# Inner rows of a gated layer transposed by VectorE and placed by transfers, with one buffer for split queries and keys

## The chip, the core and the metric

The kernel runs on one core of a Trainium2 chip. The metric is the device time of one execution in microseconds. The engines are TensorE (PE; its weight loads are listed apart as PEld), VectorE (DVE), ScalarE (ACT), GpSimd (POOL) and SyncE (SP), which here only issues transfers.

## What is computed

Block-causal attention over 8 batches, 8 heads, 576 positions and 64 dimensions a head (blocks of 64), whose result, 4608 rows of 512, goes through a gated layer with 1024 inner columns:

```python
scores = scale * np.matmul(q, k.transpose(0, 1, 3, 2))
mask = block_i >= block_j
scores = np.where(mask, scores, -1000000000.0)
scores = scores - np.max(scores, axis=-1, keepdims=True)
attn = np.exp(scores)
attn = attn / (np.sum(attn, axis=-1, keepdims=True) + 1e-09)
out = np.matmul(attn, v)                      # then rows of all heads side by side: x
h = x @ w_in
e = np.exp(h - np.max(h, axis=-1, keepdims=True))
sm = e / (np.sum(e, axis=-1, keepdims=True) + 1e-09)
solu = h * sm
mu = np.mean(solu, axis=-1, keepdims=True)
var = np.mean((solu - mu) ** 2, axis=-1, keepdims=True)
ln = (solu - mu) / np.sqrt(var + 1e-06) * g_ln
return ln @ w_out
```

q, k and v are float32; w_in and w_out come as 64-bit floats, whose words the kernel turns into float32 itself.

## The kernel before, in words

Matmul operands are split into a high part (a copy rounded to the matmul's type) and a low part (the difference), and three products of parts are summed, so each product below is three matmuls. The work has two streams.

*Attention*, `attention(p)`, for 32 pairs of heads (4 pairs a batch). Keys and queries of a pair are loaded by four transfers each, in pieces of 32 floats, so that DVE's transpose of 32x32 blocks (L428) gives them with the head dimension on the partitions (`kt`, `qt`). ACT (or POOL) makes the high parts `kh`, `qh` (L429, L430), DVE the low parts `ql`, `kl` (L432, L434); these four exist twice, for even and odd pairs. POOL copies the last query block of both heads into a block-diagonal pair `qdh`, `qdl` (L439). Then come the scores on PE (64-row matmuls L458 for query blocks of 128, and L452 for the last blocks of both heads), DVE's row maxima (L481), ACT's exponentials with row sums (L485), the scaling by the reciprocal sums (L501 on POOL), 25 PE transposes of the probabilities (L512) with copies out of PSUM by ACT (L389), the product with the values (AV, L545) and its copies into `xt` (also L389), which holds three batches.

*The layer*, `moe(t, key)`, for 36 tiles of 128 rows. `xh`, `xl` are split from `xt` (L577, L581). H, the product with w_in, is two halves of 12 matmuls (L602) into one 1024-wide PSUM tile. DVE takes the maximum (L608), ACT the exponential into `u` (L609), DVE three small steps (L617 to L619) and the product with h into `u` (L610). `u` is centred (L612 on POOL or L613 on DVE), ACT squares it for the variance (L614, output into `junk`), and POOL makes the row factor (L625, L626). `u`, the inner rows, is transposed by PE, four 128x128 transposes a half (L637); ACT copies the high part `ch` out of PSUM (L641) and DVE subtracts the low part `cl` (L642). O, the product with w_out, is two halves of 12 matmuls (L650), ACT scales it into `ob` (L654), SP stores it (L656). `ub`, `ob` exist twice, `ch`, `cl` once.

The weights are made from their words in 16 pieces (`prep`), with temporaries in the third buffer of `xt`.

The order of each engine's instructions is written out by a planner, `Schedule.run`: a list scheduler over operations with assumed durations, latencies and priorities (`PARAMS`, one number for each kind of operation, added to the number of the pair or tile). It runs at build time; on the chip each engine works through its own list and waits on semaphores. `K["np"]` is the number of pairs, `e0`, `a_...` are penalties for letting another engine do an operation. PSUM is given out as two tiles of 1024 (kind D) and four of 512 (kind S).

Of the kernel before, what the change touches and what calls it, by code (L numbers as in the profile page):

```python
# [31 lines left out]
NPT = 2  # L32
SWITCH = 165.0
# [164 lines left out]
def kernel(  # L198
# [11 lines left out]
    K = PARAMS  # L210
# [16 lines left out]
    def sb(name, shape, dt=F32):  # L227
        return cp.tile([P] + shape, dt, name=name)
# [18 lines left out]
    qdh, qdl = ([sb(f"{x}{i}", [P], F32R) for i in range(2)] for x in ("qdh", "qdl"))  # L247
# [20 lines left out]
    xt = [sb(f"xt{i}", [NP, S]) for i in range(3)]  # L268
# [62 lines left out]
    xtf = xt[2].rearrange("p a b -> p (a b)")  # L331
    wtmp = [(xtf[:, 0:512], xtf[:, 512:1024], ob[0]), (xtf[:, 1024:1536], xtf[:, 1536:2048], ob[1])]
# [59 lines left out]
    def attention(p):  # L392
# [5 lines left out]
        half = [slice(0, 64), slice(64, 128)]  # L398
        for nm, src, dst in (("kz", k, kz), ("qz", q, qz)):

            def load(nm=nm, src=src, dst=dst):
                for g in range(4):
                    dma = ACT if p == 0 and nm == "kz" else SP
# [5 lines left out]
            op("SP", 1600, load, w=[nm], key=(K["l0"] if p == 0 else p) + K["ld" + sfx], tail=2400)  # L409
# [122 lines left out]
        x2 = wkeys if b0 == 2 else []  # L532
# [22 lines left out]
        for ph in range(2):  # L555
            av = avs[ph]
            for rows, parts in xparts[ph]:
                for c_, q_, l_ in parts:
                    copy(2, l_, lambda rows=rows, av=av, c_=c_, q_=q_, l_=l_: (xt[b0 % 3][rows, hp, q_ : q_ + l_], PS(av)[rows, c_ : c_ + l_]), 1.0, [("xt", b0 % 3, hp, rows.start, q_)], ke, av, x2)


    def moe(t, key):
# [51 lines left out]
        op("ACT", t_act(1024, 135), lambda: ACT.activation(junk, u, AF.Square, accum_out=m[:, 4:5]), r=[uk], w=[("m4", i)], key=key + K["sq"])  # L614
# [86 lines left out]
```

## Time and profile before

| what | value |
|---|---|
| median of 3 runs | 790.3 us (789.97 to 790.9) |
| the profiled execution | 790.35 us, its span (first to last instruction) 788.6 us |
| PE, PEld busy | 760.3 us, 595.4 us |
| DVE, ACT, POOL busy | 471.7, 521.6, 341.7 us |
| mean granted TensorE clock | 0.975 |
| transfers | 47.05 MB in 198,551 packets |

The busy time of PE is the union of records that overlap; what an instruction adds to the run is read from the chain of work that ended last, whose pieces follow each other without overlap. A group's mean duration is that of one record. Idle time of an engine counts only where that engine is what the others wait for. "Granted clock" is the share of full TensorE speed that the chip allowed in a stretch.

### The profile page before, as it was taken

The page shows a single profiled execution, that of the slowest core. Times are in us where ns is not written, and L with a number is a line of the kernel's source. Part 1 is how long each engine was busy: PE and PEld are TensorE (multiplying, and loading weights), DVE is VectorE, ACT ScalarE, POOL GpSimd, SP SyncE. Part 2 cuts the span into 40 slices and gives each one's busy share as a digit, 9 for nine tenths or more (in the row PEclk, how much of TensorE's full clock was granted, in tenths as well). Part 3 has the DMA queues.
Part 4 walks back from the last instruction along what each step waited for, and adds up shares of the span by engine and source line. Part 5 has one row for each costly group of instructions (what it writes and reads, how often), then busy time and mean ns, then how long its engine had stood idle before and what let it go on. Part 6 is the DMA issues. An engine that isn't in the chain of part 4 may idle for free.

```text
span 788.6 us, 13834 instructions
## 1 busy us (share of the span) xinstructions
PE 760.3 (96%) x4687; PEld 595.4 (76%) x4687; DVE 471.7 (60%) x1191; ACT 521.6 (66%) x1349; POOL 341.7 (43%) x593
## 2 busy tenths in 40 slices
PE   4878999999999999999999999999999999999998
PEld 3656776887777777777777777787777878888886
DVE  5889998955666555555555666655554534444442
ACT  5788989876677676666777667677666654443332
POOL 4766857645444444444444444444445131121100
PEclk8787999999999999999999999999999999999999
DMA  9764653322222222222222222222200100000001
GB/s 185 144 137 118 120 120 88 61 59 59 58 43 48 59 49 55 59 46 59 59 59 59 59 46 48 55 51 54 59 23 22 30 14 27 26 16 28 14 27 41
DMA packets 198551, 47.05 MB, mean 60 GB/s; under 512 B 191824, under 2 KB 191824, under 8 KB 198480
## 3 DMA queue, kind: packets, MB, share of 16 engines
q1 hardware_dynamic: 196112, 45.87, 26.9%
q8 instruction: 37, 0.61, 0.3%
q10 hardware_dynamic: 2368, 0.30, 0.3%
q14 instruction: 34, 0.28, 0.1%
HBM read 36.70 MB, written 9.44 MB: 59 GB/s over the span
## 4 chain that ended last, share of the span: by engine, by line
PE 86%; ACT 5%; DVE 4%; DMA 2%; issue 1%; POOL 1%; SPq 0%; DVEq 0%; ACTq 0%; POOLq 0%
PE ps L650 25%; PE ps L602 25%; PE ps L512 10%; PE ps L545 9%; PE ps L458 8%; PE ps L637 4%; PE ps L452 3%; ACT pb L485 2%; DVE nm L481 1%; DMA ub<-in_moe_w_out_dram 1%; DMA kz<-in_k_dram 1%; DMA ub<-in_moe_w_in_dram 1%; POOL pb L501 0%; ACT xt L389 0%; DVE ql L432 0%
## 5 line engine op out<-in xcount | busy, mean ns | idle before, releaser
L501 POOL TENSOR_SCALAR pb<-pb,rz 128x384 f32<-128x384 f32 (+4 forms) x288 | 176.6, 629 | 241.4 <-DVE rz L494 227.2
L485 ACT ACTIVATE pb<-ps,nm 128x256 f32<-128x256 f32 (+4 forms) x288 | 155.1, 548 | 47.3 <-DVE nm L481 46.6
L389 ACT ACTIVATE pt<-ps 128x512 f32<-128x512 f32 (+1 forms) x224 | 108.5, 562 | 42.0 <-PE ps L512 41.6
L642 DVE TENSOR_TENSOR cl<-ps,ch 128x512 fp32r<-128x512 f32 x72 | 49.4, 686 | 142.7 <-ACT ch L641 142.7
L481 DVE TENSOR_REDUCE nm<-ps 128x1 f32<-128x256 f32 (+4 forms) x288 | 131.4, 509 | 2.1 <-PE ps L452 2.1
L512 PE MATMUL ps<-ident,pb 128*128 128x128 f32 x800 | 111.2, 287 | 11.2 <-POOL pb L501 6.3
L512 PEld LDWEIGHTS ps<-ident,pb 128*128 128x128 f32 x800 | 93.9, 146 | 24.6 <-POOL pb L501 9.7
L545 PE MATMUL ps<-pt,vr 128*64 128x320 f32 (+4 forms) x896 | 93.8, 360 | 0.3 <-ACT pt L389 0.3
L545 PEld LDWEIGHTS ps<-pt,vr 128*64 128x64 f32 x896 | 59.3, 137 | 34.4 <-issue 1.3
L602 PE MATMUL ps<-wih,xh 128*128 128x512 f32 x288 | 84.7, 416 | 0.2 <-ACT pb L485 0.2
L650 PE MATMUL ps<-woh,ch 128*128 128x512 f32 x288 | 83.4, 411 | 0.0
L602 PE MATMUL ps<-wil,xh 128*128 128x512 f32 x288 | 79.8, 399 | 0.0
L650 PE MATMUL ps<-wol,ch 128*128 128x512 f32 x288 | 79.0, 396 | 0.0
L602 PE MATMUL ps<-wih,xl 128*128 128x512 f32 x288 | 78.8, 395 | 0.0
L650 PE MATMUL ps<-woh,cl 128*128 128x512 f32 x288 | 78.6, 394 | 0.0
L625 POOL TENSOR_TENSOR ms<-ms,mhalf 128x1 f32<-128x1 f32 x36 | 19.8, 549 | 131.8 <-DVE ms L622 131.7
L641 ACT ACTIVATE ch<-ps 128x512 fp32r<-128x512 f32 x72 | 44.0, 611 | 49.5 <-PE ps L637 49.5
L458 PE MATMUL ps<-kh,qh 64*128 64x256 f32 (+3 forms) x256 | 57.4, 395 | 10.5 <-POOL qh L430 5.4
L602 PEld LDWEIGHTS ps<-wil,xh 128*128 128x128 f32 x288 | 54.9, 190 | 13.0
L654 ACT ACTIVATE ob<-ps,ms 128x512 f32<-128x512 f32 x36 | 24.8, 688 | 60.0 <-PE ps L650 54.3
L602 PEld LDWEIGHTS ps<-wih,xl 128*128 128x128 f32 x288 | 54.4, 189 | 12.9
L650 PEld LDWEIGHTS ps<-wol,ch 128*128 128x128 f32 x288 | 54.3, 188 | 12.8
(83 smaller groups left out, 1275.5 us busy)
## 6 DMA issues: line engine op xcount, KB each, us to landing
qz<-in_q_dram SPq DMA_DIRECT2D x128, 72.0 KB, 2.5
out_dram<-ob SPq DMA_DIRECT2D x36, 256.0 KB, 2.0
kz<-in_k_dram SPq DMA_DIRECT2D x124, 72.0 KB, 2.5
vr<-in_v_dram SPq DMA_DIRECT2D x64, 128.0 KB, 2.6
ub<-in_moe_w_in_dram SPq DMA_DIRECT2D x8, 512.0 KB, 4.2
ub<-in_moe_w_out_dram SPq DMA_DIRECT2D x8, 512.0 KB, 3.7
vr<-in_v_dram SPq DMA_DIRECT2D x32, 32.0 KB, 2.4
kz<-in_k_dram ACTq DMA_DIRECT2D x4, 72.0 KB, 3.8
```

The source lines that it names most:

```text
L389: op("ACT", t_act(n_), lambda: ACT.activation(aps()[0], aps()[1], AF.Copy, scale=scale), r=r, w=w, key=key, ps=ps, alts=[("DVE", t_dve(n_) ...
L458: PE.matmul(PS(sps[h])[:, off : off + 128 * (i_ + 1)], w_[half[h], 128 * i_ : 128 * i_ + 128], x_[half[h], 0 : 128 * (i_ + 1)], start=n_ = ...
L481: op("DVE", t_dve(wid[u]), lambda sp=sp, off=off, u=u: DVE.tensor_reduce(out=nm_[u], in_=PS(sp)[:, off : off + wid[u]], axis=AX.X, op=ALU. ...
L485: op("ACT", t_act(wid[u], 186), lambda sp=sp, off=off, u=u, zg=zg, zc=zc: ACT.activation(pb[:, poff[u] : poff[u] + wid[u]], PS(sp)[:, off ...
L501: op("POOL", 0.836 * nn + 243, lambda b=b, nn=nn, zg=zg, zc=zc: POOL.tensor_scalar(out=pb[:, poff[b] : poff[b] + nn], in0=pb[:, poff[b] : ...
L512: PE.transpose(t[:, (s_ - c0) * P : (s_ - c0 + 1) * P], pb[:, poff[b] + j * P : poff[b] + (j + 1) * P], ident)
L545: PE.matmul(PS(avs[ph])[half[h], 64 * o_ : 64 * (o_ + n_)], vt[:, j, 64 * h : 64 * h + 64], pt_.rearrange("p s q -> p (s q)")[:, 128 * s_ ...
L602: PE.matmul(o_, a_[:, c, :], w_[:, c, s_], start=(si == 0 and c == 0), stop=(si == 2 and c == NKI - 1))
L637: PE.transpose(t_[:, c * P : (c + 1) * P], u[:, (4 * hf + c) * P : (4 * hf + c + 1) * P], ident)
L641: op("ACT", t_act(512), lambda cs=cs, cps=cps: ACT.activation(ch[:, cs, :].rearrange("p c q -> p (c q)"), PS(cps), AF.Copy), w=[("ch", hf) ...
L642: op("DVE", t_dve(512), lambda cs=cs, cps=cps: DVE.tensor_tensor(out=cl[:, cs, :].rearrange("p c q -> p (c q)"), in0=PS(cps), in1=ch[:, cs ...
L650: PE.matmul(o_, a_[:, c, :], w_[:, c, :], start=(hf == 0 and si == 0 and c == 0), stop=(hf == 1 and si == 2 and c == 7))
```

## The change

The lines of the changed kernel are numbered anew: L602 and L650 (H and O) become L640 and L705, L637 becomes L693, L458, L452, L512, L545 become L497, L491, L551, L583, the loads L404 become L425 (L414 and L419 for the first four pairs).

For tiles 6 to 33 (`PET`, `PEL`) PE no longer transposes the inner rows. DVE transposes `u` in 32x32 blocks into `zb` (L670), SP moves the 16 groups of blocks to their places in `ct` by transfers of 32 partitions x 1 KB (L675), ACT copies the high part from `ct` (L683, other engines are allowed) and DVE subtracts (L686). `zb` and `ct` exist once. For the first four pairs (`PEQ`) queries and keys are loaded as they lie, in pieces of 64 floats, their last 64 positions together in `kq`, and transposed by PE (L454, L456); ACT and DVE split them from PSUM. The split queries and keys exist once (`NQK`). Square's output goes into `ob` instead of a buffer of its own, and the temporaries of `prep` lie in `zb` and `ct`. The priorities are new.

```diff
+NQK = 1
+XB = 3
+PEQ = 4
+PET, PEL = 6, 34
...
-    "nd": 2, "ld": -112.86, "lv": 9.571, "q": 88.586, "qe": 132.144, "s": 58.329, "se": -84.684,
+    "nd": 2, "ld": -183.871, "lv": -100.446, "q": -108.839, "qe": 198.742, "s": 92.976, "se": 35.817,
...
+    kq = sb("kq", [P])
-    qh, ql, kh, kl = ([sb(f"{x}{i}", [S], F32R) for i in range(2)] for x in ("qh", "ql", "kh", "kl"))
+    qh, ql, kh, kl = ([sb(f"{x}{i}", [S], F32R) for i in range(NQK)] for x in ("qh", "ql", "kh", "kl"))
...
+    zb = sb("zb", [DFF])
+    ct = sb("ct", [4, NKO, 32])
-    junk = sb("junk", [DFF], mybir.dt.bfloat16)
...
-    wtmp = [(xtf[:, 0:512], xtf[:, 512:1024], ob[0]), (xtf[:, 1024:1536], xtf[:, 1536:2048], ob[1])]
+    wtmp = [(zb[:, 0:512], zb[:, 512:1024], ob[0]), (ctf[:, 0:512], ctf[:, 512:1024], ob[1])]
...
+                if peq:
+                    for h in range(2):
+                        dma.dma_start(
+                            dst[:, 0:512].rearrange("p (c d) -> p c d", c=4)[:, :, 64 * h : 64 * h + 64],
+                            src[b0, 2 * hp + h, 0:512, :].rearrange("(c p) d -> p c d", p=P),
+                        )
...
+        if peq:
+            pq, pk = newps("S"), newps("D")
+
+            def trans(src, ps, tail):
+                for c in range(4):
+                    PE.transpose(PS(ps)[:, c * P : (c + 1) * P], src[:, c * P : (c + 1) * P], ident)
+                if tail:
+                    PE.transpose(PS(ps)[:, 4 * P : 5 * P], kq, ident)
...
+            copy(0, S, lambda: (kh_, PS(pk)[:, 0:S]), 1.0, [("kh", iq)], ke, pk)
+            copy(0, 512, lambda: (qh_[:, 0:512], PS(pq)[:, 0:512]), 0.125, [("qh", iq, 0)], ke, pq)
...
-        op("ACT", t_act(1024, 135), lambda: ACT.activation(junk, u, AF.Square, accum_out=m[:, 4:5]), r=[uk], w=[("m4", i)], key=key + K["sq"])
+        op("ACT", t_act(1024, 135), lambda: ACT.activation(ob[i].bitcast(mybir.dt.bfloat16), u, AF.Square, accum_out=m[:, 4:5]), r=[uk], w=[("m4", i), ("ob", i)], key=key + K["sq"])
...
+        if PET <= t < PEL:
+            op("DVE", t_dve(DFF), lambda: DVE.transpose(zb.rearrange("p (r c i) -> p r c i", r=4, i=32), u.rearrange("p (c r i) -> p r c i", r=4, i=32)), r=[uk] + (wkeys if t == PET else []), w=["zb"], key=key + K["ct"])
+
+            def place():
+                for r_ in range(4):
+                    for a_ in range(4):
+                        SP.dma_start(ct[32 * r_ : 32 * r_ + 32, a_, :, :], zb[32 * a_ : 32 * a_ + 32, 256 * r_ : 256 * r_ + 256])
+
+            op("SP", 2800, place, r=["zb"], w=["ct"], key=key + K["ct"], tail=2400)
...
+            if PET <= t < PEL:
+                c_ = ct[:, :, cs, :]
+                op("ACT", t_act(512), lambda c_=c_, h_=h_: ACT.activation(h_, c_, AF.Copy), r=["ct"], w=[("ch", hf)], key=key + K["ce"],
...
+                op("DVE", t_dve(512), lambda c_=c_, h_=h_, l_=l_: DVE.tensor_tensor(out=l_, in0=c_, in1=h_.bitcast(F32), op=ALU.subtract), r=["ct", ("ch", hf)], w=[("cl", hf)], key=key + K["ce"], port=True,
...
+                continue
```

How this moves instructions is seen at three places. First PE late in the program, where only tiles are left. Before, the second half of one tile's O, the next tile's first transposes, and so on (`ps` are PSUM tiles, `ub` the inner rows, `woh`, `wol` the parts of w_out, `x4` four instructions in a row):

```order
L650 MATMUL ps_65<-woh,ch 128x512 x4
L650 MATMUL ps_65<-wol,ch 128x512 x4
L650 MATMUL ps_65<-woh,cl 128x512 x4
L637 MATMUL ps_64<-ident,ub_133 128x128 x4
L650 MATMUL ps_65<-woh,ch 128x512 x4
L650 MATMUL ps_65<-wol,ch 128x512 x4
L650 MATMUL ps_65<-woh,cl 128x512 x4
L637 MATMUL ps_66<-ident,ub_133 128x128 x4
L602 MATMUL ps_62<-wih,xh_129 128x512 x4
```

And now, at the same stage:

```order
L705 MATMUL ps_63<-woh,ch 128x512 x4
L705 MATMUL ps_63<-wol,ch 128x512 x4
L705 MATMUL ps_63<-woh,cl 128x512 x4
L705 MATMUL ps_63<-woh,ch 128x512 x4
L705 MATMUL ps_63<-wol,ch 128x512 x4
L705 MATMUL ps_63<-woh,cl 128x512 x4
L640 MATMUL ps_61<-wih,xh_124 128x512 x4
```

The transposes are gone and both halves of O follow each other. Second, SP in the middle of the program, one round before (values, a result, keys, queries, values of the next pair):

```order
L413 DMA vr_82<-in_v_dram 128x4x64 x2
L417 DMA vr_82<-in_v_dram 64x2x64
L656 DMA out_dram<-ob_138 128x512
L404 DMA kz<-in_k_dram 32x18x32 x4
L404 DMA qz<-in_q_dram 32x18x32 x4
```

and now:

```order
L675 DMA ct<-zb 32x256 x16
L434 DMA vr_84<-in_v_dram 128x4x64 x2
L438 DMA vr_84<-in_v_dram 64x2x64
L425 DMA kz<-in_k_dram 32x18x32 x4
L425 DMA qz<-in_q_dram 32x18x32 x4
L711 DMA out_dram<-ob_134 128x512
```

Sixteen transfers stand in each round between a store and the loads of values. Third, DVE in the stage of tiles alone, from one tile's block transpose to the next one's (`ms` are row values, L646 and L648 the maximum and the product of the next tile, L651 its centring, L686 the subtractions for the tile before):

```order
L670 STREAM_TRANSPOSE zb<-ub_129 128x1024
L660 TENSOR_SCALAR ms_137<-ms_137 128x1
L646 TENSOR_REDUCE ms_136<-ps_61 128x1
L655 TENSOR_SCALAR ms_136<-ms_136 128x1
L656 RECIPROCAL ms_136<-ms_136 128x1
L657 TENSOR_SCALAR ms_136<-ms_136 128x1
L648 SCALAR_TENSOR_TENSOR ub_128,ms_136<-ps_61,ub_128 128x1024
L686 TENSOR_TENSOR cl<-ct,ch 128x4x4x32
L649 TENSOR_SCALAR ms_136<-ms_136 128x1
L651 TENSOR_SCALAR ub_128<-ub_128,ms_136 128x1024
L686 TENSOR_TENSOR cl<-ct,ch 128x4x4x32
L670 STREAM_TRANSPOSE zb<-ub_128 128x1024
```

The subtractions from `ct` now stand between the product and the block transpose of the next tile.

## Rows read from the trace of the kernel before

**Rows 1.** The page's part 1: busy time, share of the span, instructions.

```profile
PE 760.3 (96%) x4687; PEld 595.4 (76%) x4687; DVE 471.7 (60%) x1191; ACT 521.6 (66%) x1349; POOL 341.7 (43%) x593
```

**Rows 2.** Stretches: start:end length, busy PE, PEld, DVE, ACT, POOL, clock, DMA share, GB/s.

```profile
0.00:40.00 40.00, 27.06 (x156) 20.61 (x156) 28.73 (x68) 25.18 (x67) 23.88 (x56) 0.79 0.85 166
40.00:136.00 96.00, 84.49 (x556) 62.94 (x554) 87.33 (x216) 85.55 (x237) 65.68 (x99) 0.89 0.53 118
136.00:590.00 454.00, 454.00 (x2955) 356.23 (x2954) 272.17 (x715) 319.21 (x855) 210.46 (x369) 1.00 0.26 53
590.00:770.00 180.00, 180.00 (x959) 143.95 (x956) 79.17 (x185) 86.73 (x186) 40.94 (x69) 1.00 0.07 23
```

**Rows 3.** Groups: the inner transposes; x count | busy us, mean ns | idle before.

```profile
L637 PE MATMUL ps<-ident,ub 128*128 128x128 f32 x288 | 44.5, 277 | 0.0
```

**Rows 4.** Chain in order of time, one round: start us, us, what.

```profile
341.14 2.98 PE ps L602 x12
...
346.19 0.44 PE ps L637 x4
...
349.96 0.59 PE ps L637 x4
...
355.93 2.78 PE ps L602 x12
...
362.58 2.99 PE ps L602 x12
```

**Rows 5.** The same view, two tiles of the last stretch.

```profile
700.29 5.59 PE ps L602 x24
...
712.36 2.79 PE ps L602 x12
```

**Rows 6.** Waits: who waited for whom, us in total, times, longest.

```profile
PEld ps L458 <- issue: 24.0, 69, 0.4
```

**Rows 7.** Groups of ACT: exponentials, their accumulator reads, copies of transposed probabilities.

```profile
L485 ACT ACTIVATE pb<-ps,nm 128x256 f32<-128x256 f32 (+4 forms) x288 | 155.1, 548 | 47.3 <-DVE nm L481 46.6
L389 ACT ACTIVATE pt<-ps 128x512 f32<-128x512 f32 (+1 forms) x224 | 108.5, 562 | 42.0 <-PE ps L512 41.6
L485 ACT ACTIVATION_READ_ACCUMULATOR pb<-ps,nm 128x1 f32 x288 | 57.9, 201 | 0.0
```

**Rows 8.** Groups: the nearest to the new operations, and those of the cycles.

```profile
L428 DVE STREAM_TRANSPOSE kt<-kz 128x576 f32<-128x576 f32 x32 | 24.8, 775 | 6.6 <-DMA kz<-in_k_dram 6.5
L577 ACT ACTIVATE xh<-xt 128x512 fp32r<-128x512 f32 x32 | 20.5, 640 | 13.5 <-PE ps L602 13.5
L358 DVE TENSOR_TENSOR wil<-xt,wih 128x512 fp32r<-128x512 f32 x5 | 3.7, 745 | 0.0
L613 DVE TENSOR_SCALAR ub<-ub,ms 128x1024 f32<-128x1024 f32 x14 | 10.6, 754 | 0.5
L608 DVE TENSOR_REDUCE ms<-ps 128x1 f32<-128x1024 f32 x36 | 43.8, 1216 | 31.1 <-PE ps L602 31.0
L609 ACT ACTIVATE ub<-ps,ms 128x1024 f32<-128x1024 f32 x36 | 41.4, 1149 | 20.1 <-DVE ms L608 20.1
L432 DVE SCALAR_TENSOR_TENSOR ql<-qt,qh 128x576 fp32r<-128x576 f32 x32 | 25.7, 803 | 0.1
```

**Rows 9.** Transfers by line: issue on SP, ns min/median/max; landing us min/median/max.

```profile
L656 SPq DMA_DIRECT2D out_dram<-ob x36: 332/370/442, 173.3 to 785.5; - x36
DMA to landing us min/median/max: 2.0/2.0/3.8
L404 SPq DMA_DIRECT2D kz<-in_k_dram x124: 311/490/1683, 7.5 to 552.9; - x124
DMA to landing us min/median/max: 1.9/2.5/5.5
L417 SPq DMA_DIRECT2D vr<-in_v_dram x32: 607/607/1679, 12.8 to 611.9; - x32
```

**Rows 10.** SP's queue in order of time, early: start us, us, instruction.

```profile
23.56 3.31 SPq L404 DMA_DIRECT2D kz<-in_k_dram  x4
```

More of the change, by code (lines that the diff above doesn't have):

```diff
@@ L267 @@
     rzt = [[sb(f"rz{i}_{g}", [6]) for g in range(2)] for i in range(2)]
-    xt = [sb(f"xt{i}", [NP, S]) for i in range(3)]
+    xt = [sb(f"xt{i}", [NP, S]) for i in range(XB)]
     xh = [sb(f"xh{i}", [NKI, P], F32R) for i in range(2)]
@@ L398, in attention @@
         half = [slice(0, 64), slice(64, 128)]
+        peq = p < PEQ
         for nm, src, dst in (("kz", k, kz), ("qz", q, qz)):
             def load(nm=nm, src=src, dst=dst):
+                dma = ACT if p == 0 and nm == "kz" else SP
+                if peq:
[4 more added lines that the diff above has]
+                        )
+                    r0 = 0 if nm == "kz" else 64
+                    SP.dma_start(
+                        kq[r0 : r0 + 64, :].rearrange("p (h d) -> p h d", h=2),
+                        src[b0, 2 * hp : 2 * hp + 2, 512:576, :].rearrange("h p d -> p h d"),
+                    )
+                    return
                 for g in range(4):
-                    dma = ACT if p == 0 and nm == "kz" else SP
                     dma.dma_start(
@@ L425, in attention @@
         ke = p + K["qe" + sfx]
-        qh_, ql_, kh_, kl_, qdh_, qdl_ = qh[i], ql[i], kh[i], kl[i], qdh[i], qdl[i]
-        for x, z, t, hi, lo, scale in (("k", kz, kt, kh_, kl_, 1.0), ("q", qz, qt, qh_, ql_, 0.125)):
+        qh_, ql_, kh_, kl_, qdh_, qdl_ = (x[p % NQK] for x in (qh, ql, kh, kl, qdh, qdl))
+        iq = p % NQK
+        if peq:
[5 more added lines that the diff above has]
+                    PE.transpose(PS(ps)[:, 4 * P : 5 * P], kq, ident)
+            op("PE", 109 * 5, lambda: trans(kz, pk, True), r=["kz", "kzq", "qzq"], key=kk, opens=pk)
+            op("PE", 109 * 4, lambda: trans(qz, pq, False), r=["qz"], key=kk, opens=pq)
+            copy(0, S, lambda: (kh_, PS(pk)[:, 0:S]), 1.0, [("kh", iq)], ke, pk)
+            copy(0, 512, lambda: (qh_[:, 0:512], PS(pq)[:, 0:512]), 0.125, [("qh", iq, 0)], ke, pq)
+            copy(0, 64, lambda: (qh_[:, 512:S], PS(pk)[:, S : S + 64]), 0.125, [("qh", iq)], ke, pk)
+            op("DVE", t_dve(S), lambda: DVE.tensor_tensor(out=kl_, in0=PS(pk)[:, 0:S], in1=kh_.bitcast(F32), op=ALU.subtract), r=[("kh", iq)], w=[("kl", iq)], key=ke, ps=pk)
+            for q0, q1, ps_, o_, k_ in ((0, 512, pq, 0, ("qh", iq, 0)), (512, S, pk, 64, ("qh", iq))):
+                op("DVE", t_dve(q1 - q0), lambda q0=q0, q1=q1, ps_=ps_, o_=o_: DVE.scalar_tensor_tensor(out=ql_[:, q0:q1], in0=PS(ps_)[:, q0 + o_ : q1 + o_], scalar=0.125, in1=qh_[:, q0:q1].bitcast(F32), op0=ALU.mult, op1=ALU.subtract), r=[k_], w=[("ql", iq, 0) if q0 == 0 else ("ql", iq)], key=ke, ps=ps_)
@@ L428, in attention @@
+        for x, z, t, hi, lo, scale in () if peq else (("k", kz, kt, kh_, kl_, 1.0), ("q", qz, qt, qh_, ql_, 0.125)):
             op("DVE", t_dve(S), lambda z=z, t=t: DVE.transpose(t, z), r=[x + "z"], w=[x + "t"], key=kk)
-            op("ACT", t_act(S), lambda t=t, hi=hi, scale=scale: ACT.activation(hi, t, AF.Copy, scale=scale), r=[x + "t"], w=[(x + "h", i)], key=ke,
+            op("ACT", t_act(S), lambda t=t, hi=hi, scale=scale: ACT.activation(hi, t, AF.Copy, scale=scale), r=[x + "t"], w=[(x + "h", iq)], key=ke,
@@ L441, in attention @@
         for x, dst, src in (("qh", qdh_, qh_), ("ql", qdl_, ql_)):
-            op("POOL", 300, lambda dst=dst, src=src: last(dst, src), r=[(x, i)], w=[(x + "d", i)], key=ke)
+            op("POOL", 300, lambda dst=dst, src=src: last(dst, src), r=[(x, iq)], w=[(x + "d", iq)], key=ke)
         for g, (kind, us, masks) in enumerate(groups):
@@ L558, in attention @@
                 for c_, q_, l_ in parts:
-                    copy(2, l_, lambda rows=rows, av=av, c_=c_, q_=q_, l_=l_: (xt[b0 % 3][rows, hp, q_ : q_ + l_], PS(av)[rows, c_ : c_ + l_]), 1.0, [("xt", b0 % 3, hp, rows.start, q_)], ke, av, x2)
+                    copy(2, l_, lambda rows=rows, av=av, c_=c_, q_=q_, l_=l_: (xt[b0 % XB][rows, hp, q_ : q_ + l_], PS(av)[rows, c_ : c_ + l_]), 1.0, [("xt", b0 % XB, hp, rows.start, q_)], ke, av)
     def moe(t, key):
@@ new lines, in moe @@
+        for hf in range(2):
+            cs = slice(hf * 4, hf * 4 + 4)
+            h_, l_ = (x[:, cs, :].rearrange("p c (a j) -> p a c j", a=4) for x in (ch, cl))
+            if PET <= t < PEL:
+                c_ = ct[:, :, cs, :]
+                op("ACT", t_act(512), lambda c_=c_, h_=h_: ACT.activation(h_, c_, AF.Copy), r=["ct"], w=[("ch", hf)], key=key + K["ce"],
+                   alts=[("POOL", 671, lambda c_=c_, h_=h_: POOL.tensor_scalar(out=h_, in0=c_, scalar1=1.0, scalar2=1.0, op0=ALU.mult, op1=ALU.mult), K["a_ch"]),
+                         ("DVE", 335, lambda c_=c_, h_=h_: DVE.tensor_copy(h_, c_), K["a_chd"])], port=True)
+                op("DVE", t_dve(512), lambda c_=c_, h_=h_, l_=l_: DVE.tensor_tensor(out=l_, in0=c_, in1=h_.bitcast(F32), op=ALU.subtract), r=["ct", ("ch", hf)], w=[("cl", hf)], key=key + K["ce"], port=True,
+                   alts=[("POOL", 1225, lambda c_=c_, h_=h_, l_=l_: POOL.tensor_tensor(out=l_, in0=c_, in1=h_.bitcast(F32), op=ALU.subtract), K["a_clo"])])
+                continue
```

29 lines of the change are left out of this document (13 added, 16 removed), and 12 rows, old and new, of the table PARAMS.

## The prediction, made before the changed kernel was run

> **What bounds the kernel now.** I read the views in this order. The page's busy times and slices first: PE is busy for 96% of the span [rows 1]. The table by stretches then shows that its idle time lies at the two ends: from 136 to 770 us PE has none, at full granted clock, while DVE, ACT and POOL are busy for 60%, 70% and 46% of the middle stretch and less in the last [rows 2]. So in these 634 us a microsecond taken out of PE's queue is a microsecond of time, as long as nobody else comes late. Before 136 us it is otherwise: DVE and ACT are both about 90% busy from 40 to 136 us, PE loses 24.5 us idle in 0 to 136, and the granted clock averages 0.79 and 0.89, so a part of the work ran at the lower of the two levels (1.2 instead of 2.4 GHz). There the other engines set the time. At the end some 5 us remain in which PE's work is not in the records and the last store leaves; the change leaves the last two tiles as they are, so that stays.
>
> What an operation costs on PE is read from the chain in order of time, not from the groups: a transpose lasts 277 ns as a record [rows 3], but four of them take 0.44 us of the chain [rows 4], since records overlap. The chain also shows what it costs to go from one kind of matmul to another (64-row scores, 64-column AV, full 128): four transposes right behind scores take 0.59 instead of 0.44, an H half right behind AV 2.98 instead of 2.79. So a change of kind costs 0.15 to 0.19, I take 0.17.
>
> **The change, part by part, on PE.** (1) Of the 72 groups of four inner transposes 56 go (tiles 6 to 33): 56 x 0.44 = 24.6 us. The first of these tiles comes behind 136 us, where PE is never idle, so all of it counts. (2) The new order has fewer changes of kind: counted over PE's whole order 176 instead of 216, two fewer in each of the twenty equal rounds (one pair of heads, one tile), as the two score groups that stood between halves of O now stand between the two halves of H. 40 x 0.17 = 6.8 us. No row shows what entering the scores costs by itself; the lower bound is 0 a change, the upper 0.35, the wait for "issue" before score weight loads (24.0 us in 69 cases) [rows 6]; that makes 0 to 14 us, and I stay with the chain's own 0.17. (3) Queries and keys of the first four pairs cost 36 new PE transposes, 36 x 0.11 = 4.0 us, in the first 90 us, where PE idles over 20; I cost them at nothing, and at 4 if PE had no idle time there. A round of 21.44 us [rows 4] should become 21.44 - 0.44 - 0.59 - 0.17 = 20.2 us, a tile of the last stretch 12.07 - 0.88 = 11.19 us [rows 5].
>
> **The start.** Loads of 256-byte instead of 128-byte pieces for four pairs, 8 DVE transposes fewer (0.77 each), but PSUM is read by ACT and DVE, and one set of split queries and keys instead of two, so pair p+1 is split only when the scores of p are done. ACT's queue ahead of the last copies of the fourth pair holds 45 instead of 51 exponentials (0.75 each with the accumulator read), 28 instead of 31 copies of transposed probabilities (0.56), but on balance 2.7 us more of weight steps and splitting: 6 x 0.75 + 3 x 0.56 - 2.7 = 3.5 us less [rows 7]. PE has by then done some 2.3 us less of the work that both kernels share. Net -1.2 us. Bounds: -7 if the 5 to 6 us that PE loses between 88 and 136 us go as well; +8 if the single buffers cost 2 us in each of four pairs.
>
> **The new way of a row.** DVE transposes u in 32x32 blocks, 1024 wide: rows have 775 ns for 576 [rows 8], scaled 1.38 us. SP issues sixteen transfers of 32 KB. No row has an on-chip transfer; the nearest are the stores of the result, one issue 0.37 and landing 2.0 us after it, the loads of keys 0.49 and 2.5, the short loads of values 0.61 an issue; the shortest issue is 0.31 [rows 9]. I take the stores, whose pieces are nearest in size: 15 x 0.37 + 2.0 = 7.55 us from first issue to last landing (bounds 15 x 0.31 + 1.9 = 6.6 and 15 x 0.61 + 2.5 = 11.7). Then a copy on ACT from SBUF (0.64) and a subtraction on DVE (0.75) per half, as before within 0.1.
>
> In a round this is covered. From the end of a tile's H to its own O lie two rounds, 40 us; the row's steps add up to 1.2 + 1.4 + 0.5 + 1.2 + 0.75 + 1.4 + 7.6 + 1.4 + 1.5 = 17 us. What matters is the order: place stands on SP behind the loads of the next keys and queries and ahead of the values; SP's round is 16 x 0.37 + 2.0 + 2.0 + 1.6 + 0.4 = 11.9 of 20.2 us, and the loads it holds up are needed a round later. ACT reaches the first copy behind the next tile's exponential, by my count some 5 us after the data land. Also covered: Square writes into the output buffer instead of its own, so it waits for the store of two tiles before; in a round that store has landed long before, in the last stretch ACT waits for it about 2 us, which it has (ACT is busy for 48% there).
>
> In the last stretch (tiles alone) the way closes a cycle, because zb and ct exist once: transpose 1.38, place P, copy 0.64, subtraction 0.75, small step 0.15, centring 0.75, second subtraction 0.75, next transpose: 4.42 + P [rows 8]. With P = 7.55 that is 11.97 against PE's 11.19. Six tiles run in this regime; they fall back by 6 x 0.78 = 4.7 us. The slack at its beginning: from the end of O(t-1) the steps to the first half of O(t+1) are 0.69 + 0.61 + 0.75 + 1.38 + 7.55 + 0.64 + 0.75 = 12.4, and PE has H, O, H = 16.8 us in between, so 4.4. Cost 0.3, taken as 0.
>
> **Sum** against the profiled execution's 790.35 us (its median is 790.3, so nothing changes for the median): 790.35 - 24.6 - 6.8 - 1.2 = 757.8, so 758.
>
> **The rivals.** (A) *The last stretch follows the transfers, not PE.* With the keys' 0.49 and 2.5, P = 9.85, the cycle 14.3, the slack 2.1 and the cost 6 x 3.08 - 2.1 = 16 us: 774. For it: this is the median over 252 loads. Against it: those have 576 pieces, a transfer here has 32. 0.20.
> (B) *Slower than before: the issues queue up.* In 20 to 36 us four loads needed 2.8 to 3.3 us [rows 10], 0.83 an issue. Then P = 15 x 0.83 + 2.5 = 15, the cycle of the last stretch 19.4, no slack but 3 short, cost 6 x 8.2 + 3 = 52 us: 810. The cycle of a round (transpose 1.4, a reduction 0.7, subtraction 0.75, P, copy 0.6, subtraction 0.7, query transpose 0.8, centring 0.9) would just reach 20.9 and bind as well. It decides from P = 12.4 on, an issue of 0.66, where the last stretch has given back the 34 us. Against it: DMA's share was 0.9 then and is 0.26 in the middle and 0.07 in the last stretch [rows 2]. 0.04. The Trainium skill, "DMA: Bandwidth & Descriptors", section Rules for kernel authors, speaks against the change: many small transfers should be made one, and under 64 KB one pays mostly overhead; its section on the anatomy of one DMA gives about 2.0 us fixed for each. Were that paid one transfer after the other, place would take an estimated 16 x 2.1 = 33 us, and 28 tiles with a cycle of 37 us would need over 1,000 us. The trace does not agree that it is paid one by one: four loads are issued within 1.95 us and each lands 2.5 us after its own issue. 0.01.
> (C) *A round is held by DVE and ACT.* With one buffer for split queries the next pair's last query block must wait: from H's end reduce 1.22, exponential 1.38, three small steps 0.53, product 1.21, low part 0.80, POOL's two casts 0.55 = 5.7 us [rows 8], against O and 25 PE transposes, 5.6 + 2.7 = 8.3 us on PE. The 2.6 us between must also hold the waits and five scalings of probabilities moved from POOL to DVE ahead of the reduction. If it falls short by 1 us, 21 rounds cost 21 us: 779. 0.12.
> (D) *The start gains its full bound:* 752. 0.08.
>
> **How the numbers follow.** The forecast as it stands (750 to 766) gets 0.55. Low end 748: D with half the upper bound of the changes of kind. High end 782: C, or A with the start's +8. Outside are B and combinations. A measurement of this kernel tells about 0.2% (1.6 us) from no change. Slower needs B or A, C and a bad start at once: 0.07; within 0.2%: 0.03; faster 0.90.
>
> **What would show it.** Right: PE without idle time from some 130 us to the end, rounds of about 20.2 us in the chain, tiles of 11.2 in the last stretch, sixteen issues in about 6 us with the copy from ct waiting for nothing but PE. Wrong: PE waiting at O for ch or cl in the last stretch (A, B), or at the 320-wide scores for POOL's casts in each round (C), or an idle time of PE before 136 us much different from 24 us (start). If PE is never idle and the round is still over 20.6 us, the price of a change of kind was wrong.

## The result and the profile after

The changed kernel takes 778.05 us (median of 4 runs, 777.28 to 779.3), the kernel before 790.13 us in the same comparison; the ratio is 0.9853, 95% interval 0.9828 to 0.9877. So it is faster by 12 us. The forecast was 758, faster by 32: the time lies within the outer range of 748 to 782, outside the 750 to 766 of the forecast as it stands, and the gain is little more than a third of what was forecast. The profiled execution took 777.44 us, its span is 775.4 us.

Part 1 of the page and the table by stretches (columns as in [rows 2]) of the changed kernel answer to [rows 1, 2]:

```profile
PE 732.9 (95%) x4499; PEld 575.1 (74%) x4499; DVE 560.7 (72%) x1375; ACT 520.7 (67%) x1347; POOL 266.9 (34%) x435
```

```profile
0.00:40.00 40.00, 29.11 (x190) 21.85 (x190) 29.59 (x76) 27.64 (x74) 23.81 (x49) 0.96 0.70 177
40.00:136.00 96.00, 84.86 (x579) 64.61 (x580) 90.53 (x227) 82.13 (x224) 52.69 (x74) 0.95 0.47 105
136.00:590.00 454.00, 452.87 (x2917) 358.06 (x2916) 347.89 (x867) 329.61 (x872) 159.60 (x262) 1.00 0.35 78
590.00:770.00 180.00, 164.48 (x811) 129.60 (x810) 92.65 (x207) 80.66 (x179) 30.78 (x51) 0.97 0.17 50
```

In the middle PE is still never idle for long, though DVE is now busy for 77% of it instead of 60%. The last row is the news: before, PE was busy for all of these 180 us at clock 1.00; now it loses 15.5 us, and the granted clock averages 0.97.

One round of the middle in the chain of waits (start us, us, what) answers to [rows 4]:

```profile
344.63 2.97 PE ps L640 x12
347.60 1.24 PE ps L497 x12
348.84 2.98 PE ps L640 x12
351.82 2.79 PE ps L705 x12
...
362.07 2.86 PE ps L583 x28
364.93 1.12 PE ps L640 x4
```

From H to H it is 364.93 - 344.63 = 20.30 us, where 20.2 were forecast, and the rounds that follow, up to 588 us, have the same length. The rounds do what was expected of them; what is missing of the gain is missing in the last stretch. Waits from 640 us on (who waited for whom, us in total, times, longest):

```profile
ACT ch L683 <- DMA ct<-zb: 50.5, 7, 8.7
DVE cl L686 <- ACT ch L683: 42.2, 7, 7.5
...
PE ps L705 <- ACT ch L683: 15.2, 5, 4.0
ACT ob L652 <- DMA out_dram<-ob: 12.6, 7, 3.0
```

The timeline of that stretch, DVE, ACT, SP and PE put together by time for one tile (in brackets the idle time before and what ended it):

```profile
705.31 0.63 ACT L683 ACTIVATE ch<-ct 128x512 fp32r<-128x512 f32 x1 [8.69 <-DMA ct<-zb]
705.97 0.69 DVE L686 TENSOR_TENSOR cl<-ct,ch 128x512 fp32r<-128x512 f32 x1 [7.51 <-ACT ch L683]
705.99 1.19 PE L705 MATMUL ps<-woh,ch 128*128 128x512 f32 x4 [2.89 <-ACT ch L683]
706.58 0.15 DVE L649 TENSOR_SCALAR ms<-ms 128x1 f32<-128x1 f32 x1
706.76 0.76 DVE L651 TENSOR_SCALAR ub<-ub,ms 128x1024 f32<-128x1024 f32 x1
707.02 1.82 PE L705 MATMUL ps<-wol,ch 128*128 128x512 f32 x4
707.43 0.69 DVE L686 TENSOR_TENSOR cl<-ct,ch 128x512 fp32r<-128x512 f32 x1
708.03 1.24 DVE L670 STREAM_TRANSPOSE zb<-ub 128x1024 f32<-128x1024 f32 x1
709.34 10.01 SPq L675 DMA_DIRECT2D ct<-zb  x16
...
720.76 0.63 ACT L683 ACTIVATE ch<-ct 128x512 fp32r<-128x512 f32 x1 [8.37 <-DMA ct<-zb]
721.44 1.21 PE L705 MATMUL ps<-woh,ch 128*128 128x512 f32 x4 [2.45 <-ACT ch L683]
```

The cycle that the prediction drew stands here. From one copy of ct to the next are 15.45 us, of which 4.03 lie before place's first issue and 11.4 are place until the copy starts; PE needs 11.2 for a tile and waits. After three of its five waits it runs for some matmuls at the lower of its two clock levels: here four take 1.82 instead of 1.10 us, at a granted clock of 0.52 from 707.0 to 710.3 us. How place gets its length shows in the row of its line (duration ns min/median/max; landing us min/median/max):

```profile
L675 SPq DMA_DIRECT2D ct<-zb x448: 507/588/1681, 220.6 to 749.6; - x150
...
DMA to landing us min/median/max: 1.7/1.8/3.5
```

The chain has the last landing of the place that begins at 709.34:

```profile
718.75 1.83 DMA ct<-zb
```

With some 0.045 us between them, an issue is 0.633 us; fifteen to the last one and 1.83 to its landing make 11.3 us, where the prediction took 7.55. The DMA engines are not what holds the issues back: their busy share is 0.17 from 709.4 to 719.4 us.

### The profile page after: what moved, and what is told of

It is laid out like the page before. It is cut to its first block, busy times and chain, and to the rows that moved or that the text cites. A ratio compares the mean times of both kernels' runs of the same rounds, so it can differ in the third digit from the quotient of the medians.

```text
span 775.4 us, 14086 instructions
## 1 busy us (share of the span) xinstructions
PE 732.9 (95%) x4499; PEld 575.1 (74%) x4499; DVE 560.7 (72%) x1375; ACT 520.7 (67%) x1347; POOL 266.9 (34%) x435
## 3 DMA queue, kind: packets, MB, share of 16 engines
q1 hardware_dynamic: 209584, 60.61, 33.5%
## 4 chain that ended last, share of the span: by engine, by line
PE 65%; DVE 9%; ACT 9%; SPq 8%; DMA 4%; issue 3%; POOL 0%; ACTq 0%; DVEq 0%
PE ps L705 20%; PE ps L640 17%; PE ps L551 10%; PE ps L583 8%; SPq L675 8%; PE ps L497 7%; ACT pb L524 3%; PE ps L491 3%; DMA out_dram<-ob 2%; DVE nm L520 1%; DMA ct<-zb 1%; ACT ob L652 1%; DVE pb L541 1%; ACT ob L709 1%; ACT xt L397 1%
## 5 line engine op out<-in xcount | busy, mean ns | idle before, releaser
L524 ACT ACTIVATE pb<-ps,nm 128x128 f32<-128x128 f32 (+4 forms) x288 | 156.1, 551 | 58.0 <-DVE nm L520 56.9
L520 DVE TENSOR_REDUCE nm<-ps 128x1 f32<-128x128 f32 (+4 forms) x288 | 133.9, 505 | 5.2 <-PE ps L491 5.2
L663 POOL TENSOR_TENSOR ms<-ms,mhalf 128x1 f32<-128x1 f32 x36 | 20.2, 562 | 305.6 <-DVE ms L660 162.7
L551 PE MATMUL ps<-ident,pb 128*128 128x128 f32 x800 | 107.0, 281 | 13.3 <-ACT pb L524 8.9
L540 POOL TENSOR_SCALAR pb<-pb,rz 128x512 f32<-128x512 f32 (+4 forms) x131 | 88.8, 692 | 79.1 <-DVE rz L533 61.9
L551 PEld LDWEIGHTS ps<-ident,pb 128*128 128x128 f32 x800 | 92.5, 144 | 29.2 <-ACT pb L524 11.2
L705 PE MATMUL ps<-woh,ch 128*128 128x512 f32 x288 | 83.0, 410 | 15.5 <-ACT ch L683 15.2
L583 PE MATMUL ps<-pt,vr 128*64 128x320 f32 (+4 forms) x896 | 93.8, 360 | 2.1 <-ACT pb L524 2.1
L583 PEld LDWEIGHTS ps<-pt,vr 128*64 128x64 f32 x896 | 59.2, 137 | 36.4 <-ACT pb L524 2.3
L640 PE MATMUL ps<-wih,xh 128*128 128x512 f32 x288 | 84.2, 413 | 0.0
L705 PE MATMUL ps<-wol,ch 128*128 128x512 f32 x288 | 81.0, 404 | 0.0
L705 PE MATMUL ps<-woh,cl 128*128 128x512 f32 x288 | 80.2, 401 | 0.0
L640 PE MATMUL ps<-wil,xh 128*128 128x512 f32 x288 | 78.9, 396 | 0.0
L640 PE MATMUL ps<-wih,xl 128*128 128x512 f32 x288 | 78.3, 393 | 0.0
L647 ACT ACTIVATE ub<-ps,ms 128x1024 f32<-128x1024 f32 x36 | 40.2, 1118 | 49.6 <-DVE ms L646 49.6
L705 PEld LDWEIGHTS ps<-woh,ch 128*128 128x128 f32 x288 | 52.2, 192 | 28.0 <-ACT ch L683 17.4
L541 DVE TENSOR_SCALAR pb<-pb,rz 128x256 f32<-128x256 f32 (+4 forms) x157 | 72.4, 524 | 0.2
L683 ACT ACTIVATE ch<-ct 128x512 fp32r<-128x512 f32 x56 | 35.7, 637 | 50.5 <-DMA ct<-zb 50.5
L686 DVE TENSOR_TENSOR cl<-ct,ch 128x512 fp32r<-128x512 f32 x56 | 38.1, 681 | 42.9 <-ACT ch L683 42.5
L705 PEld LDWEIGHTS ps<-wol,ch 128*128 128x128 f32 x288 | 55.6, 193 | 13.1
L705 PEld LDWEIGHTS ps<-woh,cl 128*128 128x128 f32 x288 | 55.3, 192 | 13.4 <-DVE ms L649 0.3
```

Source lines behind the costliest of these rows:

```text
L520: op("DVE", t_dve(wid[u]), lambda sp=sp, off=off, u=u: DVE.tensor_reduce(out=nm_[u], in_=PS(sp)[:, off : off + wid[u]], axis=AX.X, op=ALU. ...
L524: op("ACT", t_act(wid[u], 186), lambda sp=sp, off=off, u=u, zg=zg, zc=zc: ACT.activation(pb[:, poff[u] : poff[u] + wid[u]], PS(sp)[:, off ...
L540: op("POOL", 0.836 * nn + 243, lambda b=b, nn=nn, zg=zg, zc=zc: POOL.tensor_scalar(out=pb[:, poff[b] : poff[b] + nn], in0=pb[:, poff[b] : ...
L541: alts=[("DVE", nn / 1.92 + 128, lambda b=b, nn=nn, zg=zg, zc=zc: DVE.tensor_scalar(out=pb[:, poff[b] : poff[b] + nn], in0=pb[:, poff[b] : ...
L551: PE.transpose(t[:, (s_ - c0) * P : (s_ - c0 + 1) * P], pb[:, poff[b] + j * P : poff[b] + (j + 1) * P], ident)
L583: PE.matmul(PS(avs[ph])[half[h], 64 * o_ : 64 * (o_ + n_)], vt[:, j, 64 * h : 64 * h + 64], pt_.rearrange("p s q -> p (s q)")[:, 128 * s_ ...
```

## The experiments

Theory 1 says that the missing 20 us lie in this cycle; theory 2, that it is closed by Square's wait for the store of the buffer it now writes into (the chain of waits runs through that store); theory 3, that they lie at the start or in the rounds. Ratios are against the kernel before in the same comparison, with 95% intervals.

**Half of the transfers in the last stretch.** In place, for tiles 27 to 33:

```diff
-                    for a_ in range(4):
+                    for a_ in range(2 if t >= 27 else 4):
```

> Edit: the tiles of the last stretch (27 to 33) issue only 8 of the 16 transfers of the transposed row; the rest of their pieces of ct keep old values, so those rows of the output are left wrong. Everything else and the order stand. Theory 1 (the last stretch runs in the cycle transpose, sixteen issues on one queue, landing, copy, subtraction, next transpose, 15.5 us a tile, while PE needs 11.2): place shrinks from 11.35 to 8 x 0.63 + 1.85 = 6.9 us, the cycle to 11.0, PE sets the pace again, and PE's waits for ch behind 640 us (15.4 us) and the some 5 us of lower granted clock around them go: 778 - 20 = 758 us (756 to 762). Theory 2 (the cycle is closed by Square's wait for the store that reads the same output buffer): 8 issues fewer do not touch it, 772 to 779. Theory 3 (the time is lost at the start or in the rounds, not in the last stretch): 777 to 779.

Measured: 755.54 us, 0.9576 (0.9558 to 0.9594), 0.5 below the range. PE waits for nobody behind 640 us. Two stretches (columns as in [rows 2]), of the changed kernel and then of this run:

```profile
640.00:700.00 60.00, 56.49 (x260) 44.76 (x259) 26.92 (x51) 22.59 (x44) 8.21 (x13) 0.97 0.16 49
700.00:752.00 52.00, 40.55 (x158) 31.34 (x156) 18.85 (x36) 13.73 (x24) 4.71 (x8) 0.93 0.17 51
```

```profile
640.00:700.00 60.00, 60.00 (x284) 48.22 (x283) 32.00 (x58) 27.46 (x52) 10.30 (x16) 1.00 0.13 43
700.00:752.00 52.00, 49.75 (x223) 40.16 (x221) 23.61 (x47) 18.79 (x33) 4.26 (x9) 1.00 0.12 42
```

Fewer issues bring back all of it, so theory 3 is out. This is also the time that the change has when PE sets the pace to the end: 755.5, where the prediction had 758.

**Square into its own buffer.**

```diff
-ACT.activation(ob[i].bitcast(mybir.dt.bfloat16), u, AF.Square, ...)
+ACT.activation(junk, u, AF.Square, ...)
```

> Edit: Square writes into a buffer of its own again, as before the change, so that it no longer waits for the store of two tiles before; the order is kept. Theory 1: Square's wait is a follower of the late O, not a part of the cycle: 776.5 to 779 us, the tiles of the last stretch still 15.5 us apart. Theory 2: the wait (15.2 us over 10 tiles) goes, and with it most of the loss: 760 to 768 us.

Measured: 778.7 us, 0.9871 (0.985 to 0.9892). Nothing changes: Square no longer waits for the store, and the places still begin 15.4 to 15.7 us apart. Theory 2 is out: the store stood beside the cycle and was only as late as O made it.

**The last stretch back on PE.**

```diff
-PET, PEL = 6, 34
+PET, PEL = 6, 28
```

> Edit: tiles 28 to 33 are transposed by PE again (the upper tile bound of the new way is 28 instead of 34); start and rounds keep the change. Theory 1: the last stretch goes back to PE's pace with 12.07 instead of 11.19 us a tile: 778 - 20.4 + 6 x 0.88 = 763 us (760 to 767). Theory 2: Square still waits for the store; the added transposes only add: 778 + 5 = 783 us. Theory 3: 783 us as well.

Measured: 761.11 us, 0.9645 (0.9627 to 0.9662): one number takes 17 us off the changed kernel, by giving up the new way for six tiles.

**Two pairs of buffers.**

```diff
+        zk, ck, zb, ct = "zb", "ct", zb0, ct0
+        if 28 <= t < PEL and t % 2 == 0:
+            zk, ck = "zb1", "ct1"
+            zb = xt[2].rearrange("p a b -> p (a b)")[:, 0:1024]
+            ct = xt[2].rearrange("p a b -> p (a b)")[:, 1024:2048].rearrange(...)
...
```

> Edit: from tile 28 on, even tiles use a second pair of zb and ct, laid into the attention buffer of a batch that nobody reads any more; sixteen issues a tile stay. Theory 1: the copy and subtractions no longer stand between two tiles' transfers; what is left is the queue, 16 x 0.63 + 0.4 = 10.5 us a tile, below PE's 11.19: 756 to 762 us. If the order written by the planner, which counts place with 2.8 us, still makes one tile wait for another, some of the 20 us stay: 762 to 770. Theory 2: 776 to 779. Theory 3: 777 to 779.

Measured: 778.46 us, 0.9862 (0.9841 to 0.9884), a miss. Its timeline of DVE tells why (here L692 is the subtraction, L676 the transpose):

```profile
699.12 0.08 DVE L648 DVE_READ_ACCUMULATOR ub<-ps,ub 128x1 f32 x1
706.75 0.69 DVE L692 TENSOR_TENSOR cl<-xt,ch 128x512 fp32r<-128x512 f32 x1 [7.54 <-ACT ch L689]
707.36 0.15 DVE L649 TENSOR_SCALAR ms<-ms 128x1 f32<-128x1 f32 x1
707.54 0.75 DVE L651 TENSOR_SCALAR ub<-ub,ms 128x1024 f32<-128x1024 f32 x1
708.21 0.69 DVE L692 TENSOR_TENSOR cl<-xt,ch 128x512 fp32r<-128x512 f32 x1
708.81 1.24 DVE L676 STREAM_TRANSPOSE zb<-ub 128x1024 f32<-128x1024 f32 x1
```

The next tile's row is ready for centring at 699.2 and its zb is free, but DVE keeps the planned order, and there the centring and the transpose stand behind the subtraction that waits for the landing. The planner counts place with 2.8 us, by which the landing would be long past; that this is why it put them there is tested by the next two runs. So buffers alone do not open the cycle; the order closes it too.

**The true price for the planner**, with one pair of buffers and with two:

```diff
-            op("SP", 2800, place, r=["zb"], w=["ct"], key=key + K["ct"], tail=2400)
+            op("SP", 10000, place, r=["zb"], w=["ct"], key=key + K["ct"], tail=1900)
```

> Edit: one number that only the planner reads: place is counted with 10.0 us on SP's queue and 1.9 us of landing, as measured, instead of 2.8 and 2.4. What is issued stays; the planned order then puts the centring and the transpose of the next tile ahead of the two subtractions of the present one on DVE in the last stretch. Theory 1 in its sharper form (the two-buffer run suggests that it is the order on DVE, the next tile's centring and transpose behind the subtraction that waits for the landing, which closes the cycle of 15.5 us): with one buffer the cycle becomes place and landing 11.35, transpose 1.24, the two subtractions 1.4: 14.0 us; seven tiles behind PE's 11.2 by 2.8, less the some 10 us of slack that the changed kernel showed (7 x 4.3 = 30 lost 20): 768 us (763 to 771). Theory 1 in its first form (only the buffers and the queue count, the order does not): 776 to 779.

Measured: 771.37 us, 0.9772 (0.9749 to 0.9795), 0.4 above the range. The order on DVE did change: the next tile's centring begins at 685.49 us, ahead of the two subtractions, which begin at 690.45. SP's timeline of this run shows places some 14.1 us apart, as worked out, and PE still waits:

```profile
677.55 10.02 SPq L675 DMA_DIRECT2D ct<-zb  x16
687.67 0.53 SPq L711 DMA_DIRECT2D out_dram<-ob  x1
691.72 10.00 SPq L675 DMA_DIRECT2D ct<-zb  x16
```

```profile
PE ps L705 <- ACT ch L683: 11.1, 2, 5.9
```

> Edit: the true price of place for the planner together with the second pair of zb and ct from tile 28 on. Theory 1 sharper: neither order nor buffers hold the next place back, only the queue with 10.0 us of issues and a store of 0.4 in a tile of PE's 11.2: 758 us (755 to 761). First form: the price alone does nothing and the buffers alone did nothing, so 776 to 779.

Measured: 763.71 us, 0.9677 (0.9655 to 0.9699), above the range. The order counts: with it the second pair is worth 7.7 us, without it nothing. 758 is missed by 5.7, since one wait at O stays. SP's last two places:

```profile
714.10 10.63 SPq L681 DMA_DIRECT2D xt<-xt  x16
724.83 0.53 SPq L717 DMA_DIRECT2D out_dram<-ob  x1
725.45 10.01 SPq L681 DMA_DIRECT2D ct<-zb  x16
```

And PE's only long wait:

```profile
PE ps L711 <- ACT ch L689: 4.8, 1, 4.8
```

The last one stands in the queue behind the one before and a store, lands some 23 us after 714.1, and PE, whose planned order has no H left to put between, waits 4.8 us for it.

**Every other tile by PE** in the last stretch, with the order as planned:

```diff
-        if PET <= t < PEL:
+        if PET <= t < PEL and (t < 27 or t % 2):
```

> Edit: from tile 27 on only odd tiles go the new way, even ones are transposed by PE. Theory 1 in both forms: a place has two tiles of PE's time, over 22 us, for a cycle of 15.5, so it is covered; three tiles (28, 30, 32) cost 0.88 us of PE each: 3 x 0.88 less than with all of 28 to 33 on PE (761.1): 758.5 us (756 to 761). If the in-order queues of DVE and ACT make a tile that PE transposes wait behind a subtraction that waits for a landing, some of it stays: 762 to 770.

Measured: 758.49 us, 0.9607 (0.9581 to 0.9632), and no wait of PE behind 600 us. The same 15.5 us, given two tiles of PE's time, cost nothing.

**Place over DRAM.**

```diff
-                for r_ in range(4):
-                    for a_ in range(4):
-                        SP.dma_start(ct[32 * r_ : 32 * r_ + 32, a_, :, :], zb[32 * a_ : 32 * a_ + 32, 256 * r_ : 256 * r_ + 256])
+                SP.dma_start(dz, zb)
+                for r_ in range(4):
+                    SP.dma_start(ct[32 * r_ : 32 * r_ + 32, :, :, :], dz.rearrange("(a q) (r f) -> r q a f", a=4, r=4)[r_])
```

> Edit: place goes over DRAM for all 28 tiles: one transfer of the whole transposed tile to a scratch array, then four that read it back with the pieces in their places; 5 issues instead of 16, the second kind waiting for the first to land. From the rows: 0.37 and 2.0 for the write as for a store, then three issues of 0.6 and a landing of 2.0 to 2.5: P = 6.2 to 6.7 us instead of 11.35. Theory 1: the cycle is 15.5 - 4.9 = 10.6 us, under PE's 11.2: 757 us (755 to 761). If a small transfer's landing rather than its issue sets the price, P is 8 to 9 us, the cycle 12.5 to 13: 759 to 764.

Measured: 755.92 us, 0.9575 (0.9551 to 0.9598): the best complete version, 22 us faster than the changed kernel and 33 than the one before. From SP's timeline:

```profile
672.70 0.34 SPq L674 DMA_DIRECT2D dz<-zb  x1
675.34 1.75 SPq L676 DMA_DIRECT2D ct<-dz  x4
681.12 0.36 SPq L712 DMA_DIRECT2D out_dram<-ob  x1
683.86 0.34 SPq L674 DMA_DIRECT2D dz<-zb  x1
```

And from ACT's, the copy of ct:

```profile
679.87 0.63 ACT L684 ACTIVATE ch<-ct 128x512 fp32r<-128x512 f32 x1 [2.63 <-DMA ct<-dz]
```

In this tile the copy of ct starts at 679.87, so P is 7.2 us, a little over the expected 6.7, and the next place begins 11.2 us after this one, PE's own pace. The data travel twice, through DRAM, and arrive 4 us sooner. The Trainium skill, "DMA: Bandwidth & Descriptors", section Rules for kernel authors, asks for few large transfers instead of many small ones. With the direction of that rule these runs agree. The 2.0 us fixed for each transfer, which the prediction took from that page's section on the anatomy of one DMA, are given there for transfers that GpSimd issues; here SP issues them. Nor do these runs show such a cost paid one after the other: the issues follow each other every 0.63 us while a landing takes 1.8.

**No tile the new way.** `PET, PEL = 36, 36`, the rest of the change kept.

> Edit: all 36 tiles are transposed by PE, none goes the new way; one set of split queries and keys, the loads of the first four pairs and the priorities stay as in the changed kernel. PE changes the kind of matmul 179 times (176 in the changed kernel, 216 before). Theory 1: what the new way is worth where it is covered is 0.44 us for each of 56 groups, against the 755.7 us of the runs in which the last stretch follows PE: 755.7 + 24.6 + 3 x 0.17 = 781 us (778 to 784), so within 3 us of the changed kernel's 778. If a group costs its records' 4 x 0.277 = 1.1 us: 818 us. If DVE and ACT held the rounds, so that PE's transposes were hidden: 756 to 765.

Measured: 780.29 us, 0.9875 (0.9856 to 0.9895). Against 755.54 the 56 groups cost 24.75 us, 0.44 each; but PE waits for ACT, DVE and POOL in this run's middle, 3.5 us in all, 0.6 in the run compared with, so the price of the groups alone is nearer 0.39. The new way as it was written, over all 28 tiles, is worth hardly more than none (780.29 to 778.05, with intervals that overlap).

**More changes of kind** (weight -200 instead of -137, place over DRAM).

> Edit on the version that places over DRAM (755.9 us): the planner's weight for staying with a kind of matmul is -200 instead of -137, by which PE changes kind 237 instead of 176 times with the same matmuls. At 0.17 us a change, the step of the prediction: 755.9 + 61 x 0.17 = 766 us (763 to 769). At 0 a change: 756. At the upper bound of 0.35: 777. PE without idle time between 136 us and the end is needed for the reading; where it waits, its waits are taken off.

Measured: 784.17 us, 0.9922 (0.9903 to 0.9941), above the upper bound. But PE is no longer always busy in the middle:

```profile
136.00:590.00 454.00, 443.00 (x2756) 335.50 (x2755) 335.06 (x849) 315.40 (x824) 136.81 (x223) 1.00 0.37 92
```

It is idle for 11.0 us there, 0.9 in the run compared with. Taking 10.1 off the 28.3 leaves 18.2 us for 61 changes, 0.30 each; with so many operations moved that is no clean price, and the run is inconclusive on it.

**The old loads of the first four pairs** (`PEQ = 0`, place over DRAM).

> Edit on the version that places over DRAM (755.9 us): the first four pairs are loaded in 128-byte pieces and transposed by DVE, as before the change; PE loses 36 transposes at the start and changes kind 162 times (14 fewer, 2.4 us by the prediction's price). If the new loads and PE transposes are what brings the fourth pair's results 7 us earlier than before the change (78.5 instead of 85.5 us): 755.9 + 7 - 2.4 = 760.5 us (758 to 764). If they cost as much as they give, as the prediction's net of -1.2 us has it: 753 to 756.

Measured: 764.69 us, 0.9678 (0.9659 to 0.9698), just above the range: without the new loads and PE's transposes the kernel is 8.8 us slower, in spite of 14 changes of kind fewer. But the reason that was expected is not the one: the AV group of the fourth pair begins at 74.92 us here and at 75.11 with the new loads. The fifth falls back (93.09 against 84.15), in an order that the planner has written anew. Most of the loss lies in 100 to 136 us, first the version with the new loads, then this run:

```profile
100.00:136.00 36.00, 33.77 (x225) 26.32 (x225) 33.59 (x85) 29.19 (x77) 16.89 (x23) 0.95 0.28 51
```

```profile
100.00:136.00 36.00, 25.09 (x151) 18.74 (x148) 32.34 (x75) 27.26 (x69) 17.20 (x22) 0.81 0.33 72
```

**Price and weight together** on the version over DRAM (place counted as measured, weight +60).

> Edit on the version that places over DRAM: the planner counts place with 4.4 us on SP's queue and 2.8 of landing, as that way was measured, and the weight for a kind is +60, by which PE changes kind 169 instead of 176 times. At 0.17 a change 755.9 - 1.2 = 754.7 us; the place was already covered, so its price does nothing: 753 to 757. If more operations on DVE (1370 rows instead of 1308, POOL 281 instead of 347) make a round late: 758 to 770.

Measured: 757.86 us, 0.9592 (0.9566 to 0.9617), just above the range and 1.9 us slower than without, though the intervals overlap. PE is busy for 83.06 us in 40 to 136 us where in that version it is for 85.35; seven changes of kind less are not seen, and what each of the two numbers does this run cannot tell.

## Why the prediction was right in part, and where it failed

**Right: the transposes.** 56 x 0.44 = 24.6 us. Between the run with none of them and the run without waits are 24.75; that this comes so near is in part luck, since some 2.9 us of it are waits of PE. A cleaner pair is the run with tiles 28 to 33 back on PE and the one without waits: 5.57 us for twelve groups, 0.46 each. The chain's 0.44, not the records' 277 ns [rows 3, 4], was the price.

**Right: the rounds.** 20.30 us for 20.2; PE has no idle time worth naming in them, and rival C (a round held by DVE and ACT) did not come. Its casts and the 17 us of the way in a round are covered, although place takes 11.3 there too.

**Right in sum: changes of kind and start.** Together they were to give 8.0 us; the run without waits is 33.5 faster than the kernel before, and less 24.6 for the transposes that leaves 8.9 for both. How it divides stays open. The round gives 21.44 - 20.30 - 0.88 = 0.26 for two changes, 0.13 each, the run made for it 0.30. At the start the fourth pair's AV begins 7.1 us earlier, not 3.5, first before and then after the change:

```profile
82.64 2.92 PE L545 MATMUL ps<-pt,vr 128*64 128x256 f32 x28
```

```profile
75.58 2.92 PE L583 MATMUL ps<-pt,vr 128*64 128x256 f32 x28
```

The new loads are not what brings it forward, since without them it begins as early. Whether the priorities, the single set of split queries and keys or the place of the weights' temporaries does, no run separates; two sets with the new loads were not tried. So the sum of the two was right, and what the start owes it to is not shown.

**Failed: the price of an issue in place, and with it the term of the last stretch.** "I take the stores, whose pieces are nearest in size: 15 x 0.37 + 2.0 = 7.55 us." An on-chip transfer of 32 KB is issued in 0.59 us plus 0.045 and lands in 1.83: P = 11.3, near the upper bound of 11.7 from the short loads [rows 9]. Size was the wrong likeness to choose by: the issue of a 256 KB store took 0.37 and of these 32 KB 0.59. The formula of the cycle, 4.42 + P, was right: 4.0 and 11.4 between two copies of ct. With the right P it says six tiles x 4.5 = 27 us less a slack of 0.7, some 26; the changed kernel lost 22.5 against the run without waits, of which its trace shows 15.2 in five waits of PE and 60 x 0.03 + 52 x 0.07 = 5.4 in the lower clock. The slack was larger by some 3 us: PE still had an AV group of the last round, 2.9 us, when place of tile 27 began (647.18 and 646.72 us), which fits but was not tested. "Cost 0.3, taken as 0" is the term that failed, and rival A (P = 9.85, 774) named the place, with a P still too small. For B the prediction has a gain of 34 us to give back, where its own terms make 32.6; by these B decides from P = 12.2 on, an issue of 0.64, and the measured 0.63 lies just under it.

**Failed within it:** the slack was counted on the tile's own path alone. That the transpose of the next tile stands behind a subtraction that waits for a landing was in the rows of the planned order for DVE, and in the cycle's sum, but not seen as a choice: the planner made it with 2.8 us for place against a true 10, and the true number alone gives back 6.7 us.

**Right: Square's wait** for the store was dismissed, and taking it away does nothing.

## What to carry to other kernels

Where an operation has no row, a cycle it closes has to be worked out at both bounds of its price before one is taken; here the middle of the rows of issues would have shown a last stretch that no longer follows PE. A way that is covered in a steady round has to be checked again in the stage where the cover is gone; there it can be shortened (two large steps over DRAM), thinned (every other tile), or left out. And a planner's number for an operation is a part of the kernel: here the real price was over three times as long, and the order held waits that a second pair of buffers did not take away. Issuing the sixteen transfers from two engines' queues was not tried.

## What was not expected of the hardware

- An issue's time on SP's queue did not follow the bytes: 32 KB from SBUF to SBUF 0.59 us (median of 448), 128 KB from DRAM to SBUF 0.42 (112), 512 KB from SBUF to DRAM 0.38 (28). Nor did it depend on how many are issued in a row: eight took 4.95 us, sixteen 10.01. What does set it no run tells.
- In the first 40 us PE's granted clock was 0.79 in one execution (half of the transfers left out) and 0.96 in another (the changed kernel), with the same instructions there. PE was busy for 31.80 us at the lower and 29.11 at the higher, and the work that follows came at the same time: the AV group before the end of the start begins at 125.57 and 125.34 us. So in the changed kernel the lower clock did not hold the start; that it did not before the change either, with the 0.79 of [rows 2], is likely but not shown.
